# Attention and a mixture of experts in one kernel: where the expert weights are prepared, when heads are loaded, and who owns the side work's buffers

## The chip, the cores and the metric

The kernel runs on one core of one Trainium2 chip. A core has a matrix engine (TensorE, PE in the profile), a vector engine (DVE), a scalar engine (ACT), GpSimd (POOL) and SyncE (SP), which here issues nearly all DMAs. Each engine takes its own instructions strictly in order, so an instruction that waits holds up all that stand behind it on that engine. The metric is the device time of one execution in microseconds (us); lower is better.

## The reference

Causal attention with a decay bias, then a dense mixture of eight experts on its output. All arrays are float32.

```
scores = q @ k.T / 8                      # 4 batches, 8 heads, 576 tokens, 64 columns
cum    = cumsum(max(s, 0))
scores = where(causal, -1e9, scores + min(-(cum_i - cum_j), 0))
x      = softmax(scores) @ v              # as 2304 tokens x 512
logits = x @ w_gate; P = exp(logits - max)
8 times: P /= rowsum + 1e-9; P /= colsum + 1e-9; P *= 2304/8
out    = sum over e of P[:, e] * (relu(x @ w1[e]) @ w2[e])     # 512 -> 1024 -> 512
```

## The kernel before

**Number format.** Every operand of the large products is kept as a pair, a rounded high part (`hi`, a copy on ACT) and the rest (`lo`, a subtraction, mostly on POOL); a product takes three matmuls (hi hi, hi lo, lo hi). So each weight tile and each activation tile costs one ACT copy and one subtraction.

**Stages.** (1) *Attention*: 32 heads in 16 pairs, each pair in five query tiles, so 80 slots. `st0` to `st3` of a slot are scores and exponentials, normalisation, transposes, and the product with v. `prep_head` makes a head's operands from raw q and k on DVE and POOL. Into the slots go pieces of expert 0 for the batches already done (`stream`; a piece is half a first product or one chunk of a second). (2) *Rest of the stream*: what is left of expert 0, beside the balancing of P (`sinkhorn`). (3) *Plain stage*: experts 1 to 7 for the first third of the tokens (pair p = 0, 768 tokens). The first product uses Strassen-like sums of blocks (Winograd's form, seven block products per unit of 256 hidden columns, `step1`), the second is plain (`step2p`). (4) *Winograd stage*: pairs 1 and 2, both products with seven block products (`step1`, `step2`).

**Side work.** The seven-product form needs sums of weight blocks and of token blocks. `w1_prep` (attention, experts' first four units) and `w1_ahead` (plain stage, the other 24 units of the 28) build the seven operands of a unit of w1 and store them in DRAM (`w1d`) for pairs 1 and 2. In the plain stage `w1_fetch` reads the four units back, and `w1_ahead` builds a unit while the one before it is multiplied. `prep_w2` splits two w2 tiles of a unit and makes three sums, which go to DRAM (`w2d`). `x_sums` reads raw token blocks of a pair from DRAM (`xd`), makes the sums S1 to S4 and stores them; for pairs 0 and 1 it runs on POOL in the attention, for pair 2 on DVE in the plain stage, from the third expert on (lines 1164 to 1166 and 1185).

**Buffers.** Tiles with one tag share a ring of buffers. Tag `raw` has two buffers, one head's q and k (lines 331 to 338): `load_head(h + 1)` is issued right behind `prep_head(h)` and its DMA can start only when POOL's last use of head h is over. Tag `wraw` has two buffers of the four pieces of a unit's weights. Tag `sb` (four buffers) is shared in the plain stage by the sums of w1 (lines 872 and 879), of w2 (lines 1015 and 1016) and of the tokens (line 284); those of w2 and of the tokens come free only when their DMA store has landed.

**Order.** A scheduler puts each engine's instructions in order when the kernel is built, from the program's order and its own estimates; on the chip that order is fixed. Memory of a pool that was closed is reused by later ones.

Of the kernel before, what the change touches and what calls it, by code (L numbers as in the profile page):

```python
# [46 lines left out]
def fused_kernel(ctx: ExitStack, tc: tile.TileContext, qT, kT, v, s, w_gate, wu, out):  # L47
# [36 lines left out]
    def spill(b):  # L84

        for blk in range(2 * NTP):
            lo, hi = max(GB[b], blk * TP), min(GB[b + 1], (blk + 1) * TP)
            if lo >= hi:
                continue
# [1 line left out]
            for j in range(2):
                for hl in range(2):
                    nc.sync.dma_start(
                        out=xd[p, f"{i + 1}{j + 1}"][:, hl, :, lo - blk * TP : hi - blk * TP],
                        in_=xg[b][hl][:, 2 * j : 2 * j + 2, lo - GB[b] : hi - GB[b]].bitcast(F32),
                    )
# [144 lines left out]
    def w1_prep(pool, u):  # L241

        r = pool.tile([P, KD, 2, P], F32, name="sa", tag="sa")
        nc.sync.dma_start(out=r.rearrange("p k f c -> p (k f c)"), in_=wu[u, :, 0:1024])
# [24 lines left out]
        nc.sync.dma_start(out=w1d[u], in_=w7.bitcast(F32))
        yield  # L270

    def x_sums(pool, p, k, th, n, eng):
# [6 lines left out]
        ta = pool.tile([P, n], F32, name="sc", tag="sc", bufs=2)  # L279
        tb = pool.tile([P, n], F32, name="sc", tag="sc", bufs=2)  # L280
        pend = []

        def parts(o, src):
            t = pool.tile([P, 2, n], F32R, name="sb", tag="sb", bufs=4)
            nc.scalar.copy(t[:, 0], src)
            sub(t[:, 1], src, t[:, 0].bitcast(F32), eng)
            pend.append((o, t))

        def store():
            for o, t in pend:  # L290
                nc.sync.dma_start(out=xd[p, o][:, :, k, ts], in_=t.bitcast(F32))
            pend.clear()

        add(ta, x[:, 2, 0], x[:, 2, 1], eng)
        add(tb, x[:, 3, 0], x[:, 3, 1], eng)
        add(tb, ta, tb, eng)
        parts("S1", tb)
# [965 lines left out]
```

## Time and profile before

| what | value |
|---|---|
| median of three runs | 1814.08 us (1810.9 to 1814.54) |
| the profiled execution | 1815.05 us, span 1813.3 us |
| PE busy | 1713.0 us, 94% of the span |
| DVE, ACT, POOL busy | 1211.8, 845.2, 852.0 us |
| mean granted TensorE clock | 0.979 of 2.4 GHz |
| DMA | 359.45 MB, mean 198 GB/s |

The span runs from the first to the last instruction; the execution has 1.75 us around it. PE's matmuls overlap, so "busy" covers short delays between them: at full pace the number of matmuls started in a stretch is the better measure. The attention lasts until about 412 us, the rest of the stream until 485, the plain stage until 957, the Winograd stage to the end.

### The profile page before, as it was taken

Reading aid. Unit: us, or ns where it says so; the run is one execution under the profiler, and the core shown is the slowest. Engines: PE = TensorE matmul, PEld = TensorE weight load, DVE = VectorE, ACT = ScalarE, POOL = GpSimd, SP = SyncE. Lnnn points to the kernel's source line nnn. Section 1 sums busy time; section 2 is a strip of 40 time slices with the busy share of each in tenths; the row PEclk is TensorE's granted clock in tenths of the full one; section 3 lists DMA queues with packets and bytes.
Section 4 is the critical chain, followed back from the end, with each engine's and each line's share of the span. In section 5 each row is a group of like instructions: output and inputs, shape, how many; then the busy total and the mean of one; then the engine's idle time right before and its main releaser. Section 6 shows DMA issues by size and latency. Waiting matters only on the chain.

```text
span 1813.3 us, 31303 instructions
## 1 busy us (share of the span) xinstructions
PE 1713.0 (94%) x11109; PEld 1592.5 (88%) x11109; DVE 1211.8 (67%) x2340; ACT 845.2 (47%) x1849; POOL 852.0 (47%) x739
## 2 busy tenths in 40 slices
PE   5879988999999998989999999999999999999998
PEld 4667776788888997879879999999999999999998
DVE  6756536665545555675635877777777777777775
ACT  5775546662333434334324444444444544444442
POOL 4775562650325443444421554455445445454545
PEclk9889999999999999999999999999999999999999
DMA  6785744648456666685677655665587755655562
GB/s 164 210 263 177 213 130 116 201 135 314 152 201 222 206 218 202 230 272 202 211 254 231 189 180 181 185 188 178 181 281 226 235 180 177 195 181 180 179 194 94
DMA packets 206555, 359.45 MB, mean 198 GB/s; under 512 B 19328, under 2 KB 101248, under 8 KB 205856
## 3 DMA queue, kind: packets, MB, share of 16 engines
q1 hardware_dynamic: 206080, 356.86, 61.9%
q8 instruction: 89, 1.46, 0.3%
q10 hardware_dynamic: 320, 0.59, 0.1%
q14 instruction: 66, 0.54, 0.1%
HBM read 257.28 MB, written 94.81 MB: 194 GB/s over the span
## 4 chain that ended last, share of the span: by engine, by line
PE 61%; DVE 14%; DMA 13%; issue 4%; POOL 4%; ACT 2%; SPq 2%; DVEq 0%; POOLq 0%; ACTq 0%
PE c L946 25%; PE zz L1104 11%; PE zz L1053 9%; PE y L1104 7%; DVE s L922 3%; DMA w2d<-sb 3%; DMA rawq<-qT 2%; PE g L169 2%; PE g L140 2%; DVE h L236 2%; DVE sb L236 2%; DMA sa<-xd 1%; PE sc L458 1%; DVE h L911 1%; PE pv L560 1%
## 5 line engine op out<-in xcount | busy, mean ns | idle before, releaser
L236 POOL TENSOR_TENSOR w2o<-r,w2o 128x512 fp32r<-128x512 f32 x196 | 280.1, 1452 | 386.9 <-ACT w2o L1087 386.9
L946 PE MATMUL c<-xS,w1o 128*128 128x384 f32 x1344 | 277.8, 339 | 3.4 <-DVE z L239 1.6
L1104 PE MATMUL zz<-w2o,h 128*128 128x256 f32 x2016 | 280.1, 282 | 0.0
L1104 PEld LDWEIGHTS zz<-w2o,h 128*128 128x128 f32 x2016 | 269.4, 188 | 0.4 <-ACT h L910 0.2
L1053 PE MATMUL zz<-w2p,h 128*128 128x512 f32 x1008 | 249.6, 395 | 7.7 <-ACT w2p L104 4.4
L910 ACT ACTIVATE h<-z 128x384 fp32r<-128x384 f32 x252 | 130.8, 525 | 238.8 <-DVE z L239 236.1
L922 DVE SCALAR_TENSOR_TENSOR s<-z,s 128x384 f32<-128x384 f32 x224 | 207.2, 963 | 49.0 <-ACT s L982 47.4
L946 PEld LDWEIGHTS c<-xS,w1o 128*128 128x128 f32 x1344 | 226.5, 188 | 7.5 <-DVE z L239 2.8
L1053 PEld LDWEIGHTS zz<-w2p,h 128*128 128x128 f32 x1008 | 189.3, 189 | 44.1 <-ACT w2p L104 5.0
L1104 PE MATMUL y<-w2o,h 128*128 128x256 f32 x1512 | 206.2, 283 | 3.8 <-DVE a L1039 3.0
L1104 PEld LDWEIGHTS y<-w2o,h 128*128 128x128 f32 x1512 | 196.4, 188 | 8.5 <-DVE a L1039 7.3
L946 PE MATMUL c<-x,w1o 128*128 128x384 f32 x1008 | 202.0, 336 | 0.0
L911 DVE SCALAR_TENSOR_TENSOR h<-z,h 128x384 fp32r<-128x384 f32 x252 | 168.6, 676 | 49.2 <-ACT h L910 46.1
L236 POOL TENSOR_TENSOR h<-s,h 128x384 fp32r<-128x384 f32 x112 | 137.9, 1235 | 87.7 <-ACT h L918 86.9
L239 DVE TENSOR_TENSOR z<-c,t 128x384 f32<-128x384 f32 x252 | 135.4, 549 | 59.6 <-PE c L946 56.6
L946 PEld LDWEIGHTS c<-x,w1o 128*128 128x128 f32 x1008 | 171.2, 188 | 0.1
L1039 DVE SCALAR_TENSOR_TENSOR a<-zz,prob,a 128x256 f32<-128x256 f32 (+1 forms) x210 | 110.2, 530 | 82.8 <-PE zz L1104 53.0
L918 ACT CAST h<-s 128x384 fp32r<-128x384 f32 x224 | 113.2, 514 | 94.2 <-DVE s L922 92.9
L946 PE MATMUL c<-xS,wp 128*128 128x384 f32 x672 | 133.8, 341 | 4.3 <-DVE z L239 3.5
L1087 ACT CAST w2o<-r 128x1024 fp32r<-128x1024 f32 x98 | 102.4, 1046 | 59.1 <-PE y L1104 49.1
L946 PEld LDWEIGHTS c<-xS,wp 128*128 128x128 f32 x672 | 121.4, 192 | 9.5 <-DVE z L239 4.4
L236 DVE TENSOR_TENSOR h<-s,h 128x384 fp32r<-128x384 f32 x112 | 122.3, 1111 | 0.1
(152 smaller groups left out, 2844.0 us busy)
## 6 DMA issues: line engine op xcount, KB each, us to landing
w1o<-w1d SPq DMA_DIRECT2D x392, 256.0 KB
w1d<-wp SPq DMA_DIRECT2D x72, 512.0 KB
r<-wu SPq DMA_DIRECT2D x70, 512.0 KB
r<-w2d SPq DMA_DIRECT2D x56, 512.0 KB
sa<-wu SPq DMA_DIRECT2D x28, 512.0 KB
w2d<-sb SPq DMA_DIRECT2D x56, 256.0 KB
wraw<-wu SPq DMA_DIRECT2D x44, 256.0 KB
rawq<-qT SPq DMA_DIRECT2D x64, 144.0 KB
```

The lines of the kernel that those rows point to most:

```text
L140: nc.tensor.matmul(ps[:, :n], lhsT=w1[:, w, o : o + P], rhs=xcols(b, x, k, n0, n), start=(k == 0 and t == 0), stop=(k == KD - 1 and t == 2),)
L236: (eng or nc.gpsimd).tensor_tensor(out=out, in0=a, in1=b, op=ALU.subtract)
L239: (eng or nc.gpsimd).tensor_tensor(out=out, in0=a, in1=b, op=ALU.add)
L910: nc.scalar.activation(t[:, 0], z, AF.Relu)
L911: nc.vector.scalar_tensor_tensor(out=t[:, 1], in0=z, scalar=0.0, in1=t[:, 0].bitcast(F32), op0=ALU.max, op1=ALU.subtract,)
L918: nc.scalar.copy(t[:, 0], z)
L922: nc.vector.scalar_tensor_tensor(out=out, in0=z, scalar=0.0, in1=other, op0=ALU.max, op1=op)
L946: nc.tensor.matmul(ps, lhsT=w[:, wl, k], rhs=x[:, xl, k], start=(fresh and k == 0 and t == 0), stop=(k == 1 and t == 2), skip_group_check= ...
L1039: nc.vector.scalar_tensor_tensor(out=a, in0=ps, scalar=prob[:, c, e : e + 1], in1=a, op0=ALU.mult, op1=ALU.add)
L1053: nc.tensor.matmul(zb[ci], lhsT=h[:, a, ci * P : (ci + 1) * P], rhs=w[:, b_], start=(ui == 0 and f == 0 and t == 0), stop=(ui == UPE - 1 a ...
L1087: nc.scalar.copy(w[:, :, 0], r)
L1104: nc.tensor.matmul(ps, lhsT=h[:, a, ci * P : (ci + 1) * P], rhs=w[:, ui, b_], start=(fresh and ui == 0 and t == 0), stop=(ui == UPE - 1 an ...
```

## The change

- **Heads**: tag `raw` has four buffers; heads are loaded two ahead. Tag `wraw` has four buffers, and all four pieces of a unit are loaded together. `lt` gets a tag of its own.
- **Spill**: the attention's output goes to DRAM in small pieces, one head pair at a time, five slots after it is done, and not one token group at a time.
- **No weights prepared in the attention**: `w1_prep` and `w1_fetch` are gone. `w1_ahead` builds all 28 units, the first one during the rest of the stream.
- **Token sums**: `x_sums` always runs on POOL, in nine small steps with tags of its own (`sx`, `sc`, `sh`); the copy, the `lo` and the store of a sum stand in later steps than the sum. Pair 0 stays in the attention (from slot 45, 192 columns). Pair 1 moves to the plain stage, from its first expert on, two calls of three, and pair 2 to the Winograd stage, both with 96 columns.
- **Own buffers in the plain stage**: `s1` for w1, `sb` (a new pool) for w2 alone. `r2` has three buffers and is loaded three ahead; `h` has 18 for 20, `w2p` 8 for 9. The scaling of the accumulators by P (`scale_acc`) is issued where an accumulator is first used, not behind its load.

```diff
-    def w1_prep(pool, u):
...
+    def x_sums(pool, p, k, th, n, xb):
...
+        x = pool.tile([P, 4, 2, n], F32, name="sx", tag="sx", bufs=xb)
         for i, o in enumerate(XRAW):
             nc.sync.dma_start(out=x[:, i], in_=xd[p, o][:, :, k, ts])
         yield
+        yield
+        t = [pool.tile([P, n], F32, name="sc", tag="sc", bufs=5) for _ in range(3)]
...
+        add(t[1], x[:, 2, 0], x[:, 2, 1])
+        add(t[0], x[:, 3, 0], x[:, 3, 1])
+        add(t[0], t[1], t[0])
+        yield
+        hi("S1", t[0])
+        sub(t[1], x[:, 0, 0], t[1])
+        add(t[1], t[1], x[:, 0, 1])
+        yield
+        lo("S1", t[0])
+        hi("S3", t[1])
...
+        store("S1")
...
     def load_head(h):
-        tag, bufs = ("raw", 2) if h else ("T", 5)
+        tag, bufs = ("raw", 4) if h else ("T", 5)
...
-    wrp = [apool, "wraw"]
+    wrp = [apool, "wraw", 4]
...
-    plan = [(0, 6, w1_prep(stage, u)) for u in range(UPE, UPE + NPRE)]
-    plan += [(44, 6, g) for g in xs(0)] + [(64, 6, g) for g in xs(1)]
+    PREP0, PREP1 = 45, NS - 4
+    xs0 = [x_sums(stage, 0, k, th, 192, 1) for k in range(2) for th in range(2)]
+    jobs = [(PREP0, g) for g in xs0 for _ in range(9)]
...
-            if h + 1 < B * H:
-                load_head(h + 1)
+            if h + 2 < B * H:
+                load_head(h + 2)
+        if 4 <= ti - 1 and slots[min(ti - 5, NS - 1)][1] == 4 and ti - 5 >= 0:
+            spill(*divmod(slots[ti - 5][0], NPAIR))
...
-            t13 = p0.tile([P, 2, 2, P], F32, name="sb", tag="sb", bufs=4)
+            t13 = p0.tile([P, 2, 2, P], F32, name="s1", tag="s1", bufs=2)
...
-        t13 = p0.tile([P, 2, DH], F32, name="sb", tag="sb", bufs=4)
+        t13 = hp[3].tile([P, 2, DH], F32, name="sb", tag="sb", bufs=4)
...
-        if 7 <= k < 11:
-            w1_fetch(0, (0, 2, 1, 3)[k - 7])
+        if k == 2:
+            w1_raw(0)
...
+        elif 12 <= k < 20 and k % 2 == 0:
+            w1_ahead(-1, (0, 2, 4, 5)[(k - 12) // 2])
...
-        [x_sums(p0, 2, k, th, 128, nc.vector) for k in range(2) for th in range(3)]
+    side = chain([x_sums(hp[3], 1, k, th, 96, 1) for k in range(2) for th in range(4)])
...
-                        if idx >= 2:
+                        nl2[0] += 1
+                        if nl2[0] % 3:
                             next(side, None)
...
+    side = chain([x_sums(hp[1], 2, k, th, 96, 1) for k in range(2) for th in range(4)])
...
+            if ci < 2:
+                next(side, None)
```

What the change makes of the order, at three places. SP, early in the attention: the loads of raw q and k (`rawq`, `rawk`) between the rows that ready head 2 (`qb_215`). Before:

```order
L336 DMA rawq<-qT 64x576
L337 DMA rawq<-qT 64x576
L336 DMA rawk<-kT 64x576
L337 DMA rawk<-kT 64x576
L634 DMA wgr<-w_gate 128x32
L415 DMA qb_215<-crow_d 4x576
L418 DMA kb<-crow_d 4x576
L428 DMA qb_215<-qa_214 64x640
L336 DMA rawq<-qT 64x576
```

Now, on the same engine:

```order
L311 DMA rawk<-kT 64x576
L312 DMA rawk<-kT 64x576
L311 DMA rawq<-qT 64x576
L312 DMA rawq<-qT 64x576
L311 DMA rawk<-kT 64x576
L312 DMA rawk<-kT 64x576
L608 DMA wgr<-w_gate 128x32
L390 DMA qb_215<-crow_d 4x576
L393 DMA kb<-crow_d 4x576
L403 DMA qb_215<-qa_214 64x640
```

Head 3 is loaded ahead of head 2's preparation, where it stood behind it.

POOL, at the start of the plain stage: `w2p` is the `lo` of a w2 tile, `wp` that of a w1 group, `w` that of expert 0's weights, `sc` and `sh` the token sums. Before:

```order
L105 TENSOR_TENSOR w_6168<-wraw,w_6168 128x512 x2
L105 TENSOR_TENSOR w2p<-r_6352,w2p 128x512 x2
L105 TENSOR_TENSOR w2p<-r_6354,w2p 128x512 x2
L105 TENSOR_TENSOR w2p<-r_6667,w2p 128x512 x2
L105 TENSOR_TENSOR w2p<-r_6682,w2p 128x512 x2
L105 TENSOR_TENSOR w2p<-r_6697,w2p 128x512
L236 TENSOR_TENSOR wp<-sa,wp 128x2x256
```

Now, on the same engine:

```order
L106 TENSOR_TENSOR w2p<-r_6227,w2p 128x512 x2
L237 TENSOR_TENSOR wp<-s_6246,wp 128x2x256
L240 TENSOR_TENSOR sc<-sx 128x96
L237 TENSOR_TENSOR wp<-sa,wp 128x2x256
L106 TENSOR_TENSOR w2p<-r_6575,w2p 128x512 x2
L240 TENSOR_TENSOR sc<-sx 128x96
L237 TENSOR_TENSOR wp<-s_6307,wp 128x2x256
L240 TENSOR_TENSOR sc<-sc 128x96
L237 TENSOR_TENSOR wp<-sa,wp 128x256
```

Groups of w1 for units 1 and 2 and the first token sums now stand between the w2 tiles, where there were w2 tiles alone.

DVE, further on in the plain stage, behind an accumulation of expert results (`a<-zz`); `z` and `h` are steps of the activation that PE waits for, `sc` and `sb<-sc` are token sums. Before:

```order
L1039 SCALAR_TENSOR_TENSOR a<-zz,prob,a 128x512
L239 TENSOR_TENSOR sc<-sa 128x128 x2
L239 TENSOR_TENSOR sc<-sc 128x128
L236 TENSOR_TENSOR sc<-sa,sc 128x128
L236 TENSOR_TENSOR sb<-sc,sb 128x128
L239 TENSOR_TENSOR sc<-sc,sa 128x128
```

Now, on the same engine:

```order
L1005 SCALAR_TENSOR_TENSOR a<-zz,prob,a 128x512 x2
L237 TENSOR_TENSOR s_6850<-s_6804,sa 128x256
L240 TENSOR_TENSOR z<-c,t 128x384 x2
L240 TENSOR_TENSOR s_6850<-s_6850,sa 128x256
L875 SCALAR_TENSOR_TENSOR h<-z,h 128x384 x2
```

The token sums are gone from DVE; the sums of w1 write `s`, a ring of their own.

## Rows read from the trace of the kernel before

**Rows 1.** Stretches: length, PE, weight loads, DVE, ACT, POOL busy, clock, DMA, GB/s.
```profile
0.00:45.00 45.00, 26.38 (x169) 21.45 (x169) 30.10 (x95) 24.60 (x70) 22.33 (x41) 0.96 0.64 165
45.00:97.00 52.00, 43.48 (x344) 35.25 (x343) 41.25 (x133) 41.57 (x118) 36.49 (x33) 0.84 0.70 209
97.00:412.00 315.00, 283.08 (x2172) 241.85 (x2173) 182.39 (x550) 187.16 (x525) 173.32 (x198) 0.95 0.58 175
412.00:485.00 73.00, 67.92 (x365) 59.18 (x363) 39.37 (x94) 19.90 (x42) 10.30 (x8) 0.95 0.64 238
485.00:540.00 55.00, 50.64 (x256) 47.43 (x255) 27.13 (x41) 22.12 (x46) 19.97 (x16) 0.94 0.61 211
540.00:675.00 135.00, 135.00 (x674) 121.36 (x674) 78.27 (x130) 54.33 (x112) 62.62 (x50) 1.00 0.63 214
675.00:810.00 135.00, 119.72 (x576) 105.52 (x575) 94.17 (x181) 53.61 (x121) 59.55 (x46) 0.97 0.73 239
855.00:940.00 85.00, 79.31 (x386) 70.24 (x385) 45.24 (x71) 28.56 (x58) 29.28 (x23) 0.98 0.68 230
957.00:1360.00 403.00, 399.78 (x2745) 395.26 (x2744) 308.19 (x480) 188.90 (x354) 186.25 (x138) 1.00 0.63 198
```

**Rows 2.** Waits in the first 45 us: who waited <- for whom, us, times, longest.
```profile
PE sc L458 <- DVE qa L434: 10.9, 1, 10.9
DVE qa L420 <- DMA rawq<-qT: 7.4, 4, 3.0
```

**Rows 3.** Groups by line, attention: names, shapes, count | busy, mean ns | idle before, releasers.
```profile
L420 DVE TENSOR_SCALAR qa<-rawq 128x512 fp32r<-128x512 f32 x16 | 11.0, 685 | 24.8 <-DMA rawq<-qT 24.4 <-POOL kb L430 0.4
L420 DVE TENSOR_SCALAR qa<-rawq 128x576 fp32r<-128x576 f32 x16 | 9.2, 574 | 10.6 <-DMA rawq<-qT 4.9 <-POOL w L105 2.6 <-DMA qb<-crow_d 2.5
L425 DVE TENSOR_SCALAR ka<-rawk,sgn 128x576 fp32r<-128x576 f32 x32 | 26.0, 813 | 8.6 <-DMA rawk<-kT 6.5 <-POOL w L105 1.6 <-POOL qa L434 0.4
L104 ACT CAST w<-wraw 128x512 fp32r<-128x512 f32 x44 | 26.4, 617 | 27.4 <-DMA wraw<-wu 27.0 <-PE g L169 0.4
L285 ACT CAST sb<-sc 128x192 fp32r<-128x192 f32 x32 | 11.1, 348 | 15.1 <-POOL sc L239 15.0
```

**Rows 4.** Order of time, start of the plain stage: start, us, engine, line [idle before].
```profile
506.21 2.29 PE L946 MATMUL c<-x,wp 128*128 128x384 f32 x6 [4.36 <-DVE h L911]
```

**Rows 5.** Order of time on DVE, the same microseconds.
```profile
505.00 0.69 DVE L236 TENSOR_TENSOR sb<-sa 128x512 f32<-128x512 f32 x1 [3.46 <-DMA w2d<-sb]
```

**Rows 6.** Groups by line, side work of the plain stage on DVE and ACT.
```profile
L239 DVE TENSOR_TENSOR sc<-sa 128x128 f32<-128x128 f32 x12 | 4.0, 332 | 15.8 <-DMA sa<-xd 15.8
L236 DVE TENSOR_TENSOR sb<-sc,sb 128x128 fp32r<-128x128 f32 x24 | 6.7, 284 | 0.8 <-ACT sb L285 0.6
L236 DVE TENSOR_TENSOR sb<-r 128x512 f32<-128x512 f32 x28 | 26.8, 957 | 9.1 <-DMA w2d<-sb 6.2 <-DMA r<-wu 2.3 <-DMA xd_S<-sb 0.6
L236 DVE TENSOR_TENSOR sb<-sb,sa 128x256 f32<-128x256 f32 x24 | 16.9, 703 | 9.1 <-DMA w2d<-sb 8.5 <-DMA xd_S<-sb 0.5
L285 ACT CAST sb<-sc 128x128 fp32r<-128x128 f32 x24 | 7.2, 299 | 30.7 <-DVE sc L239 21.9 <-issue 5.7 <-DVE sb L236 1.3
```

**Rows 7.** Groups by line, subtractions on POOL.
```profile
L236 POOL TENSOR_TENSOR w2o<-r,w2o 128x512 fp32r<-128x512 f32 x196 | 280.1, 1452 | 386.9 <-ACT w2o L1087 386.9
L236 POOL TENSOR_TENSOR h<-s,h 128x384 fp32r<-128x384 f32 x112 | 137.9, 1235 | 87.7 <-ACT h L918 86.9
L105 POOL TENSOR_TENSOR w2p<-r,w2p 128x512 fp32r<-128x512 f32 x56 | 77.5, 1399 | 92.2 <-ACT w2p L104 92.1
L236 POOL TENSOR_TENSOR wp<-sb,wp 128x512 fp32r<-128x512 f32 x48 | 66.3, 1381 | 57.9 <-ACT wp L852 56.5 <-DMA sa<-wu 1.1 <-POOL wp L236 0.4
L236 POOL TENSOR_TENSOR wp<-sa,wp 128x256 fp32r<-128x256 f32 x24 | 19.4, 807 | 39.5 <-ACT wp L852 35.2 <-issue 4.2 <-POOL w2p L105 0.2
L236 POOL TENSOR_TENSOR sb<-sc,sb 128x192 fp32r<-128x192 f32 x32 | 19.4, 610 | 6.2 <-ACT sb L285 4.9 <-PE g L140 0.9 <-DMA vt<-v 0.5
L434 POOL TENSOR_TENSOR qa<-rawq,qa 64x64 fp32r<-64x64 f32 x15 | 6.2, 414 | 0.0
```

More of the change, by code (lines that the diff above doesn't have):

```diff
@@ L82, in xcols, with spill @@
         return xgroup(b)[hl][:, k, n0 - GB[b] : n0 - GB[b] + n]
[L84 to L89, printed above, removed]
-            p, i = divmod(blk, 2)
[L91 to L96, printed above, removed]
+    def spill(b, hp):
+        lo, end = b * S, (b + 1) * S
+        j, k = divmod(hp, 2)
+        while lo < end:
+            gb = max(g for g in range(B) if GB[g] <= lo)
+            blk = lo // TP
+            hi = min(end, GB[gb + 1], (blk + 1) * TP)
+            p, i = divmod(blk, 2)
+            for hl in range(2):
+                nc.sync.dma_start(
+                    out=xd[p, f"{i + 1}{j + 1}"][:, hl, k, lo - blk * TP : hi - blk * TP],
+                    in_=xg[gb][hl][:, hp, lo - GB[gb] : hi - GB[gb]].bitcast(F32),
+                )
+            lo = hi
     wts = {}
@@ L278, in x_sums @@
         yield
[L279 to L297, printed above, removed]
-        yield
-        store()
-        sub(ta, x[:, 0, 0], ta, eng)
-        add(ta, ta, x[:, 0, 1], eng)
-        parts("S3", ta)
+        yield
+        t = [pool.tile([P, n], F32, name="sc", tag="sc", bufs=5) for _ in range(3)]
+        h = {}
+        def hi(o, src):
+            h[o] = pool.tile([P, 2, n], F32R, name="sh", tag="sh", bufs=3)
+            nc.scalar.copy(h[o][:, 0], src)
@@ L316, in x_sums @@
+        add(t[3], x[:, 1, 0], t[2])
+        add(t[3], t[3], x[:, 1, 1])
+        yield
+        store("S3")
+        lo("S2", t[2])
+        hi("S4", t[3])
+        yield
+        store("S2")
+        lo("S4", t[3])
+        yield
+        store("S4")
         yield
@@ L720, in fused_kernel @@
     )
-    wrp[:] = [late, "r2"]
+    wrp[:] = [late, "r2", 3]
     cur.update(g=ps1, gt="c")
@@ L831, in w1_group @@
         return t
-    def w1_fetch(n, g):
-        t = w1_group(n, g)
-        o, k = WGRP[g]
-        nc.sync.dma_start(out=grp[n, g].bitcast(F32), in_=w1d[unit(n)][:, o : o + k])
     def w1_store(n, g):
@@ L858, in w1_ahead @@
             return
-        if NPRE <= n + 2 < NUP and q == 0:
-            w1_raw(n + 2)
+        if q == 0:
+            if n + 2 < NUP:
+                w1_raw(n + 2)
+            if n >= 0:
+                w1_store(n, 3)
         n += 1
         if n >= NUP:
-            return
-        if n < NPRE:
-            g = {0: 0, 2: 2, 4: 1, 5: 3}.get(q)
-            if g is not None:
-                w1_fetch(n, g)
             return
@@ L1049, in step2p @@
             zb[ci] = ps2.tile([P, 512], F32, name="zz", tag="zz", bufs=3)
+        if e == 1 and ui == 1:
+            scale_acc(6 * p + 3 * i + ci)
         for f in range(NFC):
@@ L1100, in step2 @@
         fresh = o == "11" or not onz
+        if e == 1 and o in ("11", "T1"):
+            scale_acc(6 * p + (3 if o == "T1" else 0) + ci)
         for ui in range(UPE):
@@ L1145, in fused_kernel @@
     hp.insert(1, None)
-    load_r2(0)
-    load_r2(1)
+    p0bctx = ctx.enter_context(ExitStack())
+    hp.append(p0bctx.enter_context(tc.tile_pool(name="p0b", bufs=1, reuse_waits="tile")))
+    for m in range(3):
+        load_r2(m)
     NS1 = 7 * UPE
@@ L1203, in fused_kernel @@
     )
-    load_w2(0)
-    load_w2(1)
+    for i in range(3):
+        load_w2(i)
     load_acc(1)
```

101 lines of the change are left out of this document (33 added, 68 removed).

## The prediction

> **What bounds the kernel now.** I read the table of stretches first. PE is the limit from 957 us on: it idles 403 - 399.78 = 3.2 of 403 us there [rows 1]. Elsewhere it is not. In the attention it idles 18.62 + 8.52 + 31.92 = 59.1 us up to 412, of which 10.9 come before its first matmul [rows 1, 2]; 48.2 remain. No engine is full there: in 97 to 412 DVE is busy 182 and ACT 187 of 315 us [rows 1]. That is the picture of in-order engines waiting for each other, so next I read what ended their idle time. DVE waits for raw q and k 24.4 + 4.9 + 6.5 = 35.8 us, 7.4 of them on q at the start; ACT waits 27.0 us for weight pieces and 15.0 for token sums on POOL [rows 2, 3].
>
> In the plain stage the count of matmuls tells more than the busy time. At full pace PE starts 674 in 135 us, 4.99 per us, with no idle time; in 675 to 810 it starts 576, in 855 to 940 it starts 386 [rows 1]. At full pace these would take 115.4 and 77.3 us, so 19.6 and 7.7 us are lost. The first of the two is where the token sums of pair 2 run on DVE: its busy time rises from 78.27 to 94.17 of 135 us [rows 1], it waits 15.8 us for their loads, and ACT waits 21.9 us for their results [rows 6]. In the second, what shows is DVE standing at the shared ring `sb` until stores land (6.2 and 8.5 us over the stage) [rows 6]. At the stage's start one gap of PE, 4.36 us, ends when DVE gets past such a store wait of 3.46 us [rows 4, 5].
>
> **The change part by part.** The sum is made against the profiled execution, 1815.05 us; the median is 1 us below it.
>
> *Attention, loads and buffers.* With four `raw` buffers a head's load is issued one whole head earlier (the SP rows show it for head 3), so the later 35.8 - 7.4 = 28.4 us of DVE waiting should go. All four weight pieces now have a buffer each: most of ACT's 27.0 us. Of ACT's 15.0 us behind token sums, pair 1's half leaves the stage, and the copy of each sum stands a step behind it. In sum some 70 us of waits in two engines, partly beside each other. They are worth at most PE's 48.2 us of idle time, and at least nothing, if the next wait in line takes over. POOL also loses the subtractions of four w1 units and of half the token sums; DMA loses their stores. I take -30, half of the waits rounded down: these waits are spread evenly and DVE and ACT are what PE waits for, but they are not all on the path.
>
> *Spill in small pieces, 92 more DMA issues on SP* (1346 for 1254 in the order): nothing, because the token sums that read the spilled data start many slots later, and loads stand two heads ahead. If that cover fails, it is the first rival.
>
> *Rest of the stream.* PE idles 73 - 67.92 = 5.1 us there [rows 1]. The seven operands that `w1_fetch` read back ahead of the last weight pieces are replaced by a unit's raw weights, which are smaller; the first unit's four subtractions find POOL busy 10.30 of 73 us [rows 1]. I take -2, between -5.1 and +2.
>
> *Start of the plain stage.* Until now POOL had nine w2 subtractions in the first matmuls, nothing for w1. The order now has on POOL, in the first 151 matmuls (30 us at full pace), 8 `w2p` x 1.399 = 11.2, 8 wide `wp` x 1.381 = 11.0, 2 narrow x 0.807 = 1.6 and 13 token sums. A sum of 96 columns is not in the trace; it lies between 0.414 (64 columns) and 0.610 us (192) [rows 7]; I take 0.46, nearer the first, so 6.0. Together 29.8 us of 30, with six `w2p` (8.4 us) ahead of the last group of unit 1, which PE needs 11 steps in. POOL is late here: between 0 and +8.4, I take +5. The 4.36 us gap stays: the first three `prep_w2` still want six `sb` buffers of four, as before.
>
> *Plain stage.* Token sums leave DVE (78 instructions of 0.28 to 0.33 us [rows 6]) and ACT no longer stands behind them; w1's sums no longer share a ring with stores. Of the 27.3 us lost I keep 9 (the stretch 540 to 675 shows zero is reachable without token sums; some `w2d` waits remain): -18, between 0 and -27. What pays is POOL. From the first `w2p` to the last token sum of pair 1 the order has on it 22 `w2p`, 29 wide and 9 narrow `wp` and 104 sums: 30.8 + 40.0 + 7.3 + 47.8 = 125.9 us [rows 7]. Against it stand 708 matmuls, 141.8 us at 4.99 per us. Before, the same matmuls had 66.8 us of POOL beside them. So the cover is 16 us. The fewer `h` and `w2p` buffers cost nothing: four tiles of four units are alive when an expert starts, 16 of 18, and step2p frees two in the time that step1 needs for two.
>
> *Winograd stage.* The order packs pair 2's 104 sums beside 16 `w2o` and 16 `h` subtractions: 47.8 + 16 x 1.452 + 16 x 1.235 = 90.8 us of POOL [rows 7] against 726 matmuls, which at 2745 per 403 us take 106.6. Covered; with the deeper `r2` ring and later scaling I take +1, between -3.2 and +5.
>
> Sum: -30 - 2 + 5 - 18 + 1 = -44. 1815 - 44 = 1771, as a median 1770.
>
> *A rule against the change.* A subtraction of 128 columns takes 0.284 us on DVE [rows 6], one of 192 takes 0.610 us on POOL [rows 7]. The Trainium skill says under "GPSIMD Engine Reference", section "When to use GPSIMD" (Engine selection), that elementwise work belongs on VectorE, GpSimd being about twice as slow for two inputs; the rows agree. By that rule leaving the sums on DVE would be right. The stretch 675 to 810 says otherwise for this stage, because DVE holds the results PE waits for. It also says, under "SBUF — State Buffer", section "SBUF: two separate sides", that GpSimd and a VectorE instruction with two SBUF inputs exclude each other for a whole instruction. By that, as an estimate, each of the 104 sums could hold DVE up to its own length, which adds to the slower rival below. No row here separates this from DVE's other waits.
>
> **The rivals.** *The attention gains nothing* (0.20): DVE is busy 41.25 and ACT 41.57 of the 52 us from 45 to 97 [rows 1], 80% each; a removed wait then only brings the next one, and finer spills and bursts of four weight pieces hold up q and k in the queue. Against it: the raw waits are the largest single releaser of DVE's preparation of heads. Attention -3: 1798.
>
> *POOL becomes the bound of the plain stage* (0.13, slower). Its place: the first 142 us. Before, a `wp` subtraction stood idle 56.5/48 = 1.2 us on average until its ACT copy was done, a narrow one 35.2/24 = 1.5 [rows 7]. If the 60 subtractions of weights go on waiting 1.2 us each, POOL needs 125.9 + 72 = 198 for 142 us: +56, and 1815 - 30 - 2 + 5 + 1 - 18 + 56 = 1827. It decides from 16/60 = 0.27 us of wait per subtraction on. Against it: POOL was half empty and came early; when it is busy the copies are done before.
>
> *More than I take* (0.15): all idle time of the attention behind its start goes (-48) and all of the plain stage's loss (-27), start +5: 1745. The granted clock was 0.84 in 45 to 97 and 0.95 in 97 to 412, where PE paused, and 1.00 where it did not [rows 1]; if it holds, some 10 us more: 1735.
>
> *Nothing to measure* (0.05): gains and POOL's lateness cancel, 1814.
>
> **How the numbers follow.** My forecast, 1752 to 1788, has 0.47. Faster by over 0.2% (3.6 us, about what a measurement of this kernel can tell from no change): 0.47 + 0.20 + 0.15 = 0.82; within it 0.05; slower 0.13. The range reaches down to 1732 and up to 1811, so that most of the slower case and the far end of the larger gain stay outside.
>
> **What would show it.** Right: DVE's waits for `rawq` and `rawk` fall below 10 us and ACT's for `wraw` below 8; PE's idle time up to 412 us falls to some 30 and the attention ends 25 to 35 us earlier; in the plain stage no 135 us stretch starts under 640 matmuls behind its first 60 us; POOL is over 80% busy in its first 140 us and PE has waits there that POOL's `wp` ends. Wrong: the attention ends as late as before, with DVE's idle time put down to other releasers; or PE's waits for `wp` add up to more than 15 us; or the Winograd stage is longer than before by over 5 us because `w2o` comes late behind token sums.

## The result, and the profile after

The changed kernel takes 1783.11 us (median; 1782.2 to 1783.7) against 1814.31 for the kernel before in the same measurement: ratio 0.9825, 95% interval 0.9802 to 0.9849. It is 31 us faster, inside the forecast range; 44 were taken as the most likely. The profiled execution has a span of 1781.5 us (1813.3 before).

Where the 31.8 us of span went, by the first and last matmuls of each stage:

| stage | before | after | difference | predicted |
|---|---|---|---|---|
| attention (to the last product with v) | 411.8 | 385.3 | -26.5 | -30 |
| rest of the stream | 73.2 | 65.9 | -7.3 | -2 |
| plain stage, its start included | 472.4 | 464.7 | -7.6 | +5 - 18 |
| Winograd stage | 855.9 | 865.6 | +9.6 | +1 |

The stretches of the changed kernel, which answer to [rows 1] (same columns; the stages begin earlier, so the edges are moved):

```profile
0.00:45.00 45.00, 26.36 (x144) 21.61 (x144) 28.99 (x84) 22.50 (x62) 23.96 (x43) 0.92 0.70 179
45.00:97.00 52.00, 43.52 (x377) 34.79 (x378) 40.55 (x142) 42.40 (x121) 26.45 (x22) 0.93 0.63 181
97.00:385.00 288.00, 270.31 (x2160) 236.94 (x2160) 184.66 (x549) 175.56 (x495) 124.12 (x128) 0.98 0.48 141
385.00:451.00 66.00, 64.68 (x370) 56.87 (x367) 40.49 (x92) 23.56 (x49) 20.64 (x16) 1.00 0.71 265
451.00:506.00 55.00, 48.82 (x237) 44.06 (x236) 45.25 (x59) 25.61 (x57) 41.78 (x47) 0.94 0.87 283
506.00:641.00 135.00, 130.74 (x650) 116.34 (x649) 86.80 (x120) 56.34 (x131) 98.70 (x128) 1.00 0.77 247
641.00:776.00 135.00, 129.18 (x641) 115.15 (x640) 90.23 (x122) 52.41 (x109) 64.58 (x50) 1.00 0.60 205
776.00:911.00 135.00, 130.93 (x642) 115.82 (x641) 73.89 (x99) 47.54 (x95) 57.30 (x44) 1.00 0.64 217
916.00:1090.00 174.00, 164.71 (x1088) 161.32 (x1087) 128.07 (x195) 86.80 (x186) 116.80 (x154) 0.99 0.73 218
1090.00:1500.00 410.00, 407.74 (x2847) 403.89 (x2846) 313.87 (x488) 189.80 (x350) 202.66 (x150) 1.00 0.65 205
```

The attention does the same matmuls in 27 us less. PE's idle time up to its end is 385 - 26.36 - 43.52 - 270.31 = 44.8 us, against 59.1 [rows 1]; the other 12.7 us are shorter matmuls, at a clock of 0.98 for 0.95 in the long stretch. From 97 us on POOL is busy 43% (55% before), the DMA share is 0.48 (0.58 before). In the plain stage no 135 us stretch is as bad as the 576 matmuls of [rows 1], and none as good as 674. The first 174 us of the Winograd stage are new: PE is idle 9.3 us, where 957 to 1360 before lost 3.2 in 403.

The waits named by [rows 3] and [rows 6] went, and others came. Groups of the attention (to 385 us), then of the plain stage:

```profile
L395 DVE TENSOR_SCALAR qa<-rawq 128x576 fp32r<-128x576 f32 (+2 forms) x48 | 30.4, 646 | 6.6 <-DMA rawq<-qT 4.8 <-PE tr L505 1.4 <-issue 0.4
L400 DVE TENSOR_SCALAR ka<-rawk,sgn 128x576 fp32r<-128x576 f32 x32 | 21.9, 684 | 0.7 <-DMA rawk<-kT 0.7
L105 ACT CAST w<-wraw 128x512 fp32r<-128x512 f32 x36 | 20.9, 614 | 10.6 <-DMA wraw<-wu 6.1 <-PE g L170 3.8 <-issue 0.6
L255 ACT CAST sh<-sc 128x192 fp32r<-128x192 f32 x16 | 5.6, 350 | 25.4 <-POOL sc L240 22.1 <-DMA xd_S<-sh 3.3
...
L237 DVE TENSOR_TENSOR sb<-r 128x512 f32<-128x512 f32 x28 | 26.0, 928 | 29.8 <-DMA r<-wu 29.7
L875 DVE SCALAR_TENSOR_TENSOR h<-z,h 128x384 fp32r<-128x384 f32 x84 | 67.3, 810 | 22.5 <-ACT h L874 20.9
L255 ACT CAST sh<-sc 128x96 fp32r<-128x96 f32 x33 | 9.0, 271 | 32.8 <-POOL sc L240 26.8 <-DMA xd_S<-sh 5.8
L237 POOL TENSOR_TENSOR sh<-sc,sh 128x96 fp32r<-128x96 f32 x32 | 16.3, 512 | 3.8 <-ACT sh L255 3.4 <-PE c L910 0.4
```

DVE waits 5.5 us for raw q and k (35.8 before), ACT 6.1 for weight pieces (27.0). ACT still waits for POOL's sums, and longer than before: 22.1 us with half the copies. DVE's 6.2 + 8.5 us behind stores in the plain stage are gone, and with them what its other sums waited for stores. From 540 to 957 us the kernel before had in all:

```profile
DVE sb L236 <- DMA w2d<-sb: 23.9, 18, 4.0
DVE sb L236 <- DMA xd_S<-sb: 2.5, 4, 1.4
```

In their place DVE waits 29.7 us for raw w2 (2.3 before). A narrow sum on POOL takes 0.51 us (0.46 were taken).

The wait for raw w2 grew from almost nothing, and in three experts in a row it is 3.3 us long and reaches PE. One of these in order of time, on SP, DVE and PE:

```profile
743.44 0.36 SPq L985 DMA_DIRECT2D w2d<-sb  x1
743.89 0.42 SPq L965 DMA_DIRECT2D r<-wu  x1
...
749.08 0.69 DVE L237 TENSOR_TENSOR sb<-r 128x512 f32<-128x512 f32 x1 [3.42 <-DMA r<-wu]
752.49 1.01 DVE L240 TENSOR_TENSOR z<-c,t 128x384 f32<-128x384 f32 x2
...
753.10 2.35 PE L910 MATMUL c<-xS,wp 128*128 128x384 f32 x12 [1.35 <-DVE z L240]
```

SP issues the load 5.2 us before DVE gets it, directly behind the store of a sum that DVE ended at 743.4 us: the load stood in SP's order behind that store, and SP waited for DVE. Then DVE stands, the sums behind it run late, and `z`, for which PE waits, comes last. The same stands 66 us earlier and later.

As often PE waits for a DVE that hardly waits itself. Some 9 us ahead of each of these gaps stands one of 1.63 to 1.70 us:

```profile
742.47 0.94 DVE L240 TENSOR_TENSOR sb<-sb,r 128x256 f32<-128x256 f32 x1
743.33 0.74 DVE L1005 SCALAR_TENSOR_TENSOR a<-zz,prob,a 128x512 f32<-128x512 f32 x1
...
744.13 4.60 PE L1021 MATMUL zz<-w2p,h 128*128 128x512 f32 x19 [1.69 <-DVE a L1005]
```

The accumulation `a` comes late because DVE is busy with sums of w2 and an `h` in front of it.

The gap at the start of the plain stage [rows 4, 5] became two, in order of time on PE; then what DVE and POOL did ahead of the first:

```profile
460.57 2.29 PE L910 MATMUL c<-x,wp 128*128 128x384 f32 x6 [3.60 <-DVE z L240]
476.47 1.48 PE L910 MATMUL c<-x,wp 128*128 128x384 f32 x6 [2.07 <-DVE h L875]
...
454.05 1.77 DVE L237 TENSOR_TENSOR sb<-r 128x512 f32<-128x512 f32 x1
...
452.16 7.61 POOL L106 TENSOR_TENSOR w2p<-r,w2p 128x512 fp32r<-128x512 f32 x5 [2.46 <-ACT w2p L105]
```

The first gap no longer ends a wait for a store. DVE makes six sums of w2 from 452 to 460 us without a pause; five of them take 1.4 to 1.8 us beside POOL's five `w2p`, where the first, begun ahead of POOL's, took 0.68.

### The profile page after: what moved, and what is told of

It is laid out like the page before. It is cut to its first block, busy times and chain, and to the rows that moved or that the text cites. A ratio compares the mean times of both kernels' runs of the same rounds, so it can differ in the third digit from the quotient of the medians.

```text
span 1781.5 us, 31624 instructions
## 1 busy us (share of the span) xinstructions
PE 1697.2 (95%) x11109; PEld 1582.8 (89%) x11109; DVE 1241.4 (70%) x2274; ACT 844.1 (47%) x1873; POOL 916.1 (51%) x883
## 4 chain that ended last, share of the span: by engine, by line
PE 66%; DVE 13%; DMA 7%; POOL 5%; issue 4%; ACT 3%; SPq 1%; POOLq 0%; DVEq 0%; ACTq 0%
PE c L910 25%; PE zz L1074 11%; PE zz L1021 7%; PE y L1074 7%; PE g L170 3%; DVE s L886 3%; PE g L141 3%; PE pv L535 2%; DMA r<-wu 2%; PE sc L433 2%; DVE h L237 2%; PE tr L505 2%; PE c L170 2%; POOL w2p L106 2%; PE c L141 1%
## 5 line engine op out<-in xcount | busy, mean ns | idle before, releaser
L910 PEld LDWEIGHTS c<-xS,w1o 128*128 128x128 f32 x1344 | 226.8, 188 | 13.4 <-DVE z L240 8.4
L875 DVE SCALAR_TENSOR_TENSOR h<-z,h 128x384 fp32r<-128x384 f32 x252 | 179.5, 721 | 60.8 <-ACT h L874 57.5
```

The costliest lines, as they stand in the source:

```text
L875: nc.vector.scalar_tensor_tensor(out=t[:, 1], in0=z, scalar=0.0, in1=t[:, 0].bitcast(F32), op0=ALU.max, op1=ALU.subtract,)
L910: nc.tensor.matmul(ps, lhsT=w[:, wl, k], rhs=x[:, xl, k], start=(fresh and k == 0 and t == 0), stop=(k == 1 and t == 2), skip_group_check= ...
```

## The experiments

All twelve were timed beside the kernel before, four in one measurement. Their stages, from the same marks as above (us, one profiled execution each):

| kernel | attention | rest | plain | Winograd | median | ratio to before |
|---|---|---|---|---|---|---|
| heads one ahead | 379.2 | 66.0 | 465.6 | 863.9 | 1774.6 | 0.9809 (0.9789 to 0.9830) |
| before, heads two ahead | 402.1 | 76.2 | 471.3 | 855.0 | 1801.3 | 0.9941 (0.9923 to 0.9960) |
| w1 in the attention | 404.0 | 65.8 | 459.5 | 865.6 | 1794.2 | 0.9920 (0.9901 to 0.9939) |
| two piece buffers | 386.3 | 65.8 | 463.7 | 864.9 | 1781.2 | 0.9849 (0.9832 to 0.9866) |
| pair 2's sums in plain | 389.0 | 66.0 | 465.0 | 855.3 | 1775.9 | 0.9805 (0.9785 to 0.9826) |
| pair 1's sums in attention | 385.2 | 68.9 | 462.7 | 863.3 | 1781.2 | 0.9835 (0.9813 to 0.9856) |
| sums on VectorE | 387.3 | 65.9 | 468.5 | 863.3 | 1787.7 | 0.9877 (0.9852 to 0.9902) |
| ring r2 of two | 388.9 | 67.2 | 465.5 | 862.4 | 1783.0 | 0.9848 (0.9827 to 0.9870) |
| copies per batch | 386.5 | 67.8 | 460.4 | 864.6 | 1784.6 | 0.9854 (0.9838 to 0.9869) |
| sums copied at once | 385.2 | 66.9 | 461.8 | 863.2 | 1782.5 | 0.9843 (0.9826 to 0.9861) |
| sums in the w2 ring | 385.2 | 65.9 | 465.2 | 866.5 | 1783.0 | 0.9846 (0.9830 to 0.9861) |
| one ahead, pair 2 in plain | 376.1 | 65.9 | 463.4 | 858.1 | 1765.4 | 0.9746 (0.9732 to 0.9761) |

"Pair 2's sums in plain" and "sums on VectorE" have the attention of the changed kernel instruction for instruction on DVE; they end it at 389.0 and 387.3 us, the changed kernel at 385.3. So 4 us in the attention between two profiles is chance. The plain stage takes 460.4 to 465.6 us in kernels whose edit lies elsewhere. The kernel before had medians of 1811.4, 1811.8 and 1810.2 us in these three measurements and 1814.3 in that of the changed kernel, so times from different measurements compare to some 4 us. In the diffs `...` stands for lines that are not shown.

**Heads one ahead.**

```diff
-        tag, bufs = ("raw", 4) if h else ("T", 5)
+        tag, bufs = ("raw", 2) if h else ("T", 5)
...
-    load_head(3)
...
-            if h + 2 < B * H:
-                load_head(h + 2)
+            if h + 1 < B * H:
+                load_head(h + 1)
```

> The changed kernel with its heads loaded one ahead again (two raw buffers) and everything else as changed. Theory L (the attention ends 26.5 us earlier because raw q and k are there in time): VectorE's waits for rawq and rawk, 5.5 us in the changed kernel, come back to 25 to 36 us, the attention ends 10 to 15 us later (395 to 400 us for 385), the whole takes 1793 to 1798 us. Theory W (the attention gains because the preparation of four w1 units left it: POOL's subtractions, ACT's copies, the stores and loads in the queue): the waits come back in part, since the queue is emptier, 10 to 20 us, but the attention ends 0 to 4 us later, 1783 to 1787 us.

Neither: it is faster, with 1770.8 to 1776.5 us in four executions against 1780.7 to 1782.4 of "two piece buffers" in the same measurement. The waits came back only in part (21.3 us, of 35.8 before the change), and the work behind them got shorter. DVE to 379 us:

```profile
L395 DVE TENSOR_SCALAR qa<-rawq 128x576 fp32r<-128x576 f32 (+2 forms) x48 | 18.2, 408 | 20.4 <-DMA rawq<-qT 17.6 <-POOL w L106 1.8 <-DMA xd_S<-sh 1.0
L400 DVE TENSOR_SCALAR ka<-rawk,sgn 128x576 fp32r<-128x576 f32 x32 | 21.5, 672 | 6.1 <-DMA rawk<-kT 3.7 <-POOL w L106 2.4
```

The same 48 conversions take 18.2 us here and 30.4 in the changed kernel. One head of the latter in order of time, DVE and then POOL, shows why they are longer:

```profile
140.24 1.21 DVE L395 TENSOR_SCALAR qa<-rawq 128x576 fp32r<-128x576 f32 x1
141.37 0.85 DVE L400 TENSOR_SCALAR ka<-rawk,sgn 128x576 fp32r<-128x576 f32 x1
142.15 1.27 DVE L395 TENSOR_SCALAR qa<-rawq 128x64 fp32r<-128x64 f32 x1
...
139.85 1.28 POOL L409 TENSOR_TENSOR qa<-rawq,qa 64x512 fp32r<-64x512 f32 x1
141.21 0.70 POOL L240 TENSOR_TENSOR sc<-sc 128x192 f32<-128x192 f32 x1
141.87 1.49 POOL L106 TENSOR_TENSOR w<-wraw,w 128x512 fp32r<-128x512 f32 x1
```

A conversion of 64 columns takes 1.27 us: it is issued while POOL works on a weight piece and ends when POOL does (143.4 us). Where POOL is idle the three sizes take 0.19, 0.42 and 0.46 us. With the load later, POOL runs dry waiting for DVE's conversions (97.9 us in all, 59.9 in the changed kernel), and they find it idle: all 16 conversions of 64 columns take 0.18 to 0.19 us there, where in the changed kernel 10 of the 16 meet POOL.

That is why the conversions are shorter. It isn't shown to be the gain: waits and conversions of the two lines add up to 66.2 us here and to 59.6 in the changed kernel. What fell besides stands in other queues. ACT's copies of token sums and DVE's step behind ACT's `sm`, first in the changed kernel, then here:

```profile
L255 ACT CAST sh<-sc 128x192 fp32r<-128x192 f32 x16 | 5.6, 350 | 25.4 <-POOL sc L240 22.1 <-DMA xd_S<-sh 3.3
L493 DVE RECIPROCAL rec<-sm 128x2 f32<-128x2 f32 (+1 forms) x80 | 12.6, 159 | 25.8 <-ACT sm L489 25.6
```
```profile
L255 ACT CAST sh<-sc 128x192 fp32r<-128x192 f32 x16 | 5.6, 348 | 10.6 <-POOL sc L240 8.7 <-DMA xd_S<-sh 1.9
L493 DVE RECIPROCAL rec<-sm 128x2 f32<-128x2 f32 (+1 forms) x80 | 12.3, 157 | 6.7 <-ACT sm L489 6.4
```

ACT stands 13.4 us less for POOL's sums and DVE 19.2 us less for ACT. Which of these brings the gain was not separated.

**The kernel before, heads two ahead**: the same lines, the other way round.

> The kernel before with nothing changed but the heads, which are loaded two ahead (four raw buffers). Theory L: the attention ends 10 to 15 us earlier than 411.8, in all 1799 to 1804 us. Theory W: the waits for rawq and rawk fall below 10 us, and other waits take their place; the attention ends 0 to 4 us earlier, in all 1810 to 1814 us.

As theory L had it: 1801.3 us, the attention ends 9.7 us earlier. The waits for raw q and k fall to 4.6 + 0.5 us and the conversions grow here too, from 25.7 to 34.9 us:

```profile
L420 DVE TENSOR_SCALAR qa<-rawq 128x576 fp32r<-128x576 f32 (+2 forms) x48 | 34.9, 737 | 5.5 <-DMA rawq<-qT 4.6 <-issue 0.6 <-POOL qa L434 0.3
```

In the kernel before, earlier loads gain more than the longer conversions cost.

**w1 in the attention, and two piece buffers** (the reference for it).

```diff
...
+    wjobs = [g for u in range(UPE, UPE + NPRE) for g in [w1_prep(stage, u)] for _ in range(6)]
...
+        while wjobs and nw - len(wjobs) < nw * (ti - 15) // 21:
+            next(wjobs.pop(0), None)
...
```
```diff
-    wrp = [apool, "wraw", 4]
+    wrp = [apool, "wraw", 2]
...
-    def w_load_early(u, pcs=(0, 1, 2, 3)):
+    def w_load_early(u, pcs=(0, 1)):
...
+        if pc < 2:
+            w_load_early(u, (pc + 2,))
```

> The changed kernel with the w1 operands of the first four units prepared in the attention again (slots 15 to 36) and read back later, and two buffers for the weight pieces, without which it doesn't fit; so it is compared with the changed kernel that has two piece buffers. Theory W: the attention ends 10 to 18 us later than there, all of it between slots 15 and 45; the plain stage's first 60 us get 0 to 5 us shorter, because POOL has no w1 subtractions there; in all 6 to 16 us slower. Theory L: the attention ends 0 to 5 us later, and the whole is within 3 us.

> The changed kernel with two buffers for the weight pieces, pieces 2 and 3 loaded when 0 and 1 have been split, as before. If ACT's waits for weight pieces were on the path (as the sum of the prediction had it, with the 27.0 us among the 70): they come back to 15 to 25 us and the attention ends 4 to 8 us later, 1787 to 1791 us. If ACT has slack there: the waits come back, and the time stays within 2 us of the changed kernel, 1781 to 1785 us.

Preparing four units in the attention costs 404.0 - 386.3 = 17.7 us there; the plain stage is 463.7 - 459.5 = 4.2 shorter; 1794.2 for 1781.2 in all. Theory W holds, and on top of what the loads are worth in "before, heads two ahead". The 4.2 us are within what the plain stage spreads. The piece buffers are worth nothing that shows: ACT's waits come back to 14.3 us, the time stays. The attention of "w1 in the attention", then of "two piece buffers", as stretches:

```profile
0.00:404.00 404.00, 345.65 (x2682) 295.69 (x2683) 255.70 (x774) 247.80 (x694) 202.76 (x219) 0.95 0.56 167
```
```profile
0.00:386.00 386.00, 340.94 (x2681) 293.69 (x2681) 248.70 (x774) 240.88 (x678) 173.65 (x191) 0.96 0.52 151
```

PE idles 13.3 us more there; ACT, POOL and DMA carry more work, none of them full.

**Pair 2's sums in the plain stage.**

```diff
-    side = chain([x_sums(hp[3], 1, k, th, 96, 1) for k in range(2) for th in range(4)])
+    side = chain([x_sums(hp[3], p, k, th, 96, 1) for p in (1, 2) for k in range(2) for th in range(4)])
...
-                        if nl2[0] % 3:
-                            next(side, None)
+                        next(side, None)
...
-    side = chain([x_sums(hp[1], 2, k, th, 96, 1) for k in range(2) for th in range(4)])
...
-            if ci < 2:
-                next(side, None)
```

> The changed kernel with pair 2's token sums also beside the plain stage (a step of side work at every step2p), so none beside the Winograd stage. Theory S (the 9.6 us that the Winograd stage lost, 865.6 for 855.9, come from the 104 token sums on POOL that stand in its first 130 us): the Winograd stage takes 855 to 857 us again, its first two experts 85 and 60 us. Rival D (the stage lost them through the later scaling and the deeper r2 ring, whose loads collide at its start): it stays at 863 to 866 us. The plain stage, 464.7 us, has 208 sums beside it: if POOL bounds it, it gets 8 to 20 us longer; if what a sum costs is the time it takes from VectorE, 104 sums more cost what 104 cost in the Winograd stage, 6 to 11 us, and the whole stays within 4 us of the changed kernel.

Theory S. The Winograd stage takes 855.3 us, its first two experts 85.3 and 60.3 (90.2 and 65.2 in the changed kernel), and the plain stage carries 208 sums in 465.0 us: POOL doesn't bound it. The same 174 us of this kernel, PE and POOL nearly as before the change:

```profile
920.00:1094.00 174.00, 171.82 (x1159) 169.77 (x1158) 132.76 (x209) 84.28 (x162) 72.39 (x55) 1.00 0.63 193
```

DVE there, first of this kernel and then of the changed one (`h` made from `z` and from `s`, and `z`):

```profile
L875 DVE SCALAR_TENSOR_TENSOR h<-z,h 128x384 fp32r<-128x384 f32 x39 | 23.2, 603 | 7.5 <-ACT h L874 6.8
L237 DVE TENSOR_TENSOR h<-s,h 128x384 fp32r<-128x384 f32 x24 | 24.7, 1058 | 0.0
L240 DVE TENSOR_TENSOR z<-c,t 128x384 f32<-128x384 f32 x39 | 21.2, 548 | 7.2 <-PE c L910 3.6 <-ACT t L926 3.5
```
```profile
L875 DVE SCALAR_TENSOR_TENSOR h<-z,h 128x384 fp32r<-128x384 f32 x36 | 26.0, 739 | 12.3 <-ACT h L874 12.1
L237 DVE TENSOR_TENSOR h<-s,h 128x384 fp32r<-128x384 f32 x23 | 21.4, 947 | 0.7 <-ACT h L882 0.7
L240 DVE TENSOR_TENSOR z<-c,t 128x384 f32<-128x384 f32 x36 | 19.4, 547 | 7.1 <-PE c L910 6.3 <-ACT t L926 0.8
```

`h` from `z` reads two SBUF tiles and is 0.136 us longer beside the sums; `z` reads one tile from PSUM and is not. But `h` from `s`, which also reads two SBUF tiles, is 0.111 us shorter.

**Sums on VectorE**: `x_sums` gets `nc.vector` for its additions and subtractions at both places.

> The changed kernel with the token sums of pairs 1 and 2 on VectorE, at the same places, instead of POOL. Theory X (a POOL sum lengthens VectorE's instructions with two SBUF inputs, 0.55 us alone and 1.0 to 1.3 us when they meet one, and VectorE is what PE waits for): VectorE's own sums of 96 columns are 104 x 0.25 = 26 us a stage, about what POOL's take from it, so the Winograd stage stays within 4 us of 865.6 and the plain stage within 5 us of 464.7, with the mean of VectorE's h (SBUF, SBUF) back near 0.55 to 0.65 us. Rival A (ACT and w2o stand behind POOL's sums): the Winograd stage gets back to 856 to 859 us. Rival V (as the trace of the kernel before suggested: VectorE's sums hold up what PE waits for more than POOL's do): the plain stage gets 8 to 15 us longer.

`h` is back at 0.59 us in the Winograd stage, which takes 863.3 us all the same: there the engine hardly matters, as theory X said. The time of rival A (856 to 859) did not come. But this run doesn't clear ACT's order, because ACT goes on standing for the sums. DVE in those 174 us, then ACT before the copies of the sums, in the changed kernel and here:

```profile
L875 DVE SCALAR_TENSOR_TENSOR h<-z,h 128x384 fp32r<-128x384 f32 x38 | 22.0, 586 | 7.2 <-ACT h L874 7.1
L237 DVE TENSOR_TENSOR sh<-sc,sh 128x96 fp32r<-128x96 f32 x32 | 8.9, 291 | 3.5 <-ACT sh L255 3.5
```
```profile
L255 ACT CAST sh<-sc 128x96 fp32r<-128x96 f32 x31 | 8.3, 272 | 26.4 <-POOL sc L240 20.8 <-DMA xd_S<-sh 5.1
```
```profile
L255 ACT CAST sh<-sc 128x96 fp32r<-128x96 f32 x31 | 7.9, 270 | 19.3 <-DVE sc L240 6.6 <-issue 4.3 <-DMA xd_S<-sh 4.1
```

The plain stage gets 3.8 us longer, less than rival V's 8, and the whole is slower (1786.8 to 1790.6 us, against 1778.9 to 1782.7 of "pair 1's sums in attention" in the same measurement). So POOL is the better place for the sums as a whole, and in the plain stage by some 3 us or more (468.5 against 465.6 at most, one profile).

**Pair 1's sums in the attention, and the ring r2 of two.**

```diff
+    xs1 = [x_sums(stage, 1, k, th, 192, 1) for k in range(2) for th in range(2)]
+    jobs += [(64, g) for g in xs1 for _ in range(9)]
...
-    side = chain([x_sums(hp[3], 1, k, th, 96, 1) for k in range(2) for th in range(4)])
+    side = iter(())
```
```diff
...
-    wrp[:] = [late, "r2", 3]
+    wrp[:] = [late, "r2", 2]
...
-            r2[m] = late.tile([P, 2, DM], F32, name="r2", tag="r2", bufs=3)
+            r2[m] = late.tile([P, 2, DM], F32, name="r2", tag="r2", bufs=2)
...
```

> The changed kernel with pair 1's token sums in the attention again (192 columns wide, from slot 64 on) and none beside the plain stage. If a token sum costs wherever it stands, by the time it takes from VectorE and by what ACT waits for POOL: the attention ends 4 to 9 us later than 385.3, the plain stage gets 4 to 9 us shorter (456 to 461 for 464.7), and the whole stays within 4 us. If the attention's gain of 26.5 us came partly from pair 1's sums leaving it (the term of the prediction with ACT's 15.0 us): the attention ends 8 to 12 us later and the plain stage gains less than 4, 1788 to 1793 us.

> The changed kernel with two buffers in the ring r2 again, for the weight pieces of the rest of the stream and for the raw w2 of both later stages (loads two ahead). The rest of the stream takes 65.9 us in the changed kernel, 73.2 before; its VectorE and ACT waits on weight pieces went. If the ring is the reason: 70 to 73 us again. If it is what the stretch no longer has beside it (operands read back, the first token sums): 65 to 68 us. The plain stage and the Winograd stage: within 3 us of 464.7 and 865.6, unless raw w2 late is part of the Winograd stage's loss, then another 3 to 8 us.

Neither forecast for pair 1's sums came: they cost the attention nothing that shows (385.2), the rest of the stream gets 3.0 us longer, the plain stage 2.0 shorter, which is within its spread. So without a single token sum beside it the plain stage takes 462.7 us: the sums aren't what it still loses. With a ring of two the rest takes 67.2 us, not the 70 to 73 that would make the ring the reason: it is worth 1.3 us there and nothing that shows later.

**Copies per batch, sums copied at once, sums in the w2 ring**: the spill as before; `x_sums` as before but with the new tags; the parts of pair 1's sums in the ring `sb`.

> The changed kernel with the token copies to DRAM as before: a batch at once, when its attention is done, instead of a pair of heads at a time. If the small steps pay (the queue of loads isn't blocked for a burst): the attention ends 3 to 8 us later than the 385 to 389 us of kernels with the changed attention. If, as the prediction had it, nothing hangs on them: 383 to 390 us, and the whole 1779 to 1786 us.

> The changed kernel with the token sums written as before (the rounded copy on ACT and the subtraction on POOL right behind each sum, fewer steps per chunk), but with the new buffers of their own. If the form pays, since ACT's copies stand a step behind POOL's sums: ACT waits for sc more than the 22 us a stage it has now, the attention ends 3 to 6 us later, and the plain and Winograd stages get 2 to 5 us longer each, 1786 to 1794 us. If not: 1780 to 1786 us.

> The changed kernel with the rounded parts of pair 1's token sums, in the plain stage, in the ring of four that raw w2's sums use, as before the change; the rest of the side work keeps its own buffers. If own buffers are what the plain stage gained from (VectorE stood at that ring until stores had landed, 6.2 and 8.5 us): the plain stage takes 469 to 476 us for 464.7, with VectorE's waits for stores of w2d or xd back above 5 us. If moving the sums to POOL and away from w1's sums did it: within 3 us of 464.7.

None moves the time beyond the spread. With copies per batch the rest of the stream takes 1.9 us more; with the shared ring DVE waits 7.3 us for stores of the sums again, as the case for own buffers had it, but the plain stage takes 465.2 us, as the other case had it.

**Both.** Heads one ahead, and pair 2's sums in the plain stage.

> The changed kernel with heads loaded one ahead and pair 2's token sums beside the plain stage, the two edits that came out below it alone. If both gains are real and stand apart (attention 379 for 385 to 389 us, Winograd stage 855.3 for 865.6): 379 + 66 + 465 + 855.5, some 1766 us span and 1768 in all, 1764 to 1771. If the 6 us at the attention were chance (kernels whose attention is word for word the changed one's ended it between 385.3 and 389.0 us): 1772 to 1776.

1765.4 us (1762.6 to 1766.3), ratio 0.9746: the gains are real and add up. This is the fastest version, 18 us below the changed kernel and 17 to 19 below the three that were timed with it and differ little from the changed kernel.

## Why the prediction was right, and where not

The total came inside the range, and part of that is luck: the attention's term came out near for another reason than the one given, and the misses of the later terms cancelled in part.

**Attention, -30 against -26.5: right in size, wrong in cause.** The step that failed is the sum of "some 70 us of waits in two engines". By the runs, the weight pieces (27.0 us of ACT) and pair 1's sums are worth nothing that shows. The loads two ahead are worth 9.7 us in the kernel before; in the changed one they cost 6 us or more (379.2 for 385 to 389). What pays, with heads two ahead, is w1's preparation leaving the stage, 17.7 us, which the prediction put into one unpriced sentence (POOL "loses the subtractions of four w1 units", DMA "their stores"). The two parts are not independent: taken in the other order, all but the loads is worth 411.8 - 379.2 = 32.6 us, and the loads then cost. The late loads were in part a symptom of that work: with it gone and heads one ahead again the waits are 21.3 us, not 35.8. Half of the saving came as shorter matmuls rather than as PE's idle time, which fell to 44.8 us and not to 30; the granted clock over the stage is 0.96 for 0.94. That less idle time raised it is inference.

**Rest of the stream, -2 against -7.3.** Mis-sized. 3.8 us are idle time (5.1 to 1.3), the rest goes with a granted clock of 1.00 for 0.95. The term priced `w1_fetch`, and that isn't it: with it back ("w1 in the attention") the stretch takes 65.8 us. Three parts that had no price here, pair 1's sums (3.0), the copies per batch (1.9) and the ring (1.3), add up to 6.2, each from one profile.

**Start of the plain stage, +5: right in size, wrong in the wait.** The first 55 us hold 237 matmuls, 256 before [rows 1]: 19 at 4.99 per us are 3.8 us. But PE never waits there for POOL's `wp`; its 6.0 us of waits end with DVE's `z` and `h`. The gap that was to stay "as before" stays with another cause, DVE's sums beside POOL instead of a store.

**Plain stage, -18 against about -11** (7.6 and the 3.8). The step that failed is "of the 27.3 us lost I keep 9": the three later stretches still lose 674 - 650, 674 - 641 and 674 - 642 matmuls, 17.8 us at 4.99 per us. One wait was exchanged for another: for 26.4 us behind stores DVE now stands 29.7 us at raw w2. The three PE gaps behind its 3.3 us waits are 1.08, 1.35 and 1.32 us, and three more, 5.0 us in all, stand behind a DVE that hardly waits; together that is 8.8 of the 14.1 us that PE idles from 506 to 916. A ring of two in place of three changes nothing there; the load stands on SP behind a store that waits for DVE, and an earlier place wasn't tried. Sums on POOL rather than DVE are worth some 3 us or more, own buffers for the token sums nothing that shows. What the rest came from stays open: w1's sums in the old ring alone wasn't tried. The slower rival, POOL as the bound, falls: PE never waits for `wp`, POOL is busy 109.9 of the first 140 us (78%, not over 80), and 104 sums more leave the time alone. Its subtractions of weights waited 20.2 us for ACT in that stretch (14.5 for `wp`, 5.7 for `w2p`), not 72: the argument against that rival held.

**Winograd stage, +1 against +9.6: the term that was wrong.** The step that failed is "Covered": I had weighed POOL's 90.8 us of work against 106.6 us of matmuls. POOL was covered: PE waits 0.4 us for it in the stage's first 174 us. But 5.8 of PE's 9.3 us of idle time end with DVE's `z`, and the sums stand in the way of the two engines that PE does wait for. ACT stands 25.9 us in its queue for `sh` there (20.8 for POOL's sums, 5.1 for stores), in front of the copies of `h`; DVE's `h` from `z` is longer. That the sums beside this stage cost it some 10 us is shown: moved away, they take the loss with them. How they cost it is not.

The prediction gave the Trainium skill's rule ("SBUF — State Buffer", section "SBUF: two separate sides": GpSimd and a VectorE instruction with two SBUF inputs exclude each other) to the plain stage only, and said that no row separates it from other waits. The rows of after and of the experiments do: `h` from `z` takes 0.60 us without the sums and 0.74 with them, and `z` 0.55 in both. But the rule explains little of the loss. Over the same first 107 instructions with two SBUF inputs (48 `s`, 36 and 23 `h`), DVE is busy 94.3 us beside the sums and 92.0 without: what `h` from `z` loses (4.8), `h` from `s` regains by half (2.2). And on VectorE, free of it, the sums cost the stage 863.3 - 855.3 = 8.0 us as well. Both kernels have ACT standing for `sh`, 26.4 and 19.3 us, and both have more DMA beside the stage (a share of 0.73 and 0.74, 0.63 without). That points to ACT's order more than to DVE's time, but no run separates the three.

**A rule against the change.** The prediction's rows compared 128 columns on DVE with 192 on POOL. At equal width, 96 columns, the subtraction takes 0.29 us on DVE in the Winograd stage and 0.46 to 0.51 on POOL: POOL is the slower engine for a sum, and in the plain stage still the better place.

**Rivals and signs.** "The attention gains nothing" falls. Its argument, that a removed wait only brings the next one, holds for ACT: 6.1 us for pieces in place of 27.0, and 22.1 for sums in place of 15.0. Of the signs, the waits for raw q and k (5.5 us) and for pieces (6.1) and the stretches over 640 matmuls came; PE's idle time of 30 us, POOL over 80% busy and PE's waits for `wp` did not. One sign of being wrong came too, the Winograd stage over 5 us longer, though not because `w2o` was late: a single wait of PE, 0.6 us, ends with it.

## What to carry to other kernels

Before you remove a wait, ask what work made the data late, and price that work's departure: here the waits named by the profile were worth 0 to 10 us, the work behind them 18 with the loads early. Side work is not free because its engine has room: 104 sums on POOL cost the last stage some 10 us and nothing that shows in the plain stage. Look also at the queues in which its copies and conversions stand, and put it in the stage where PE already has slack. And test a prefetch again after the change that it was meant to help.
